# Four weight transfers issued during the attention stage, one ahead of the first gathers, and other places for the last expert's parts

## The chip, the cores and the metric

The kernel runs on one core of a Trainium2 chip. The metric is the device time of one execution, in microseconds (us). The core has five engines that run their own instruction streams: TensorE (PE; its weight loads are shown as PEld), VectorE (DVE), ScalarE (ACT), GpSimd (POOL) and SyncE (SP). Transfers between HBM and SBUF run on 16 DMA engines; here SP issues into the queue that the profile calls q1 and POOL into q0.

## The reference

An attention layer is followed by a mixture of experts with an early exit. What is computed, cut to what matters:

```python
# attention: batch 4, 8 heads, 768 positions, 64 columns a head
scores = scale * np.matmul(q, k.transpose(0, 1, 3, 2))
mask = retrieval heads: causal; the others: causal & (first 4 keys | last 64 keys)
a = softmax(where(mask, scores, -1e9));  attn_out = a @ v
# the rows become x: 3072 tokens x 512
do_compute = (x @ w_skip) > 0            # the other tokens are returned as they are
e_idx = argmax(xc @ w_gate);  gate_w = its softmax probability      # 8 experts
h = np.maximum(xc[mask] @ w1[e], 0.0)    # 512 -> 1024
y[mask] = gate_w[mask, None] * (h @ w2[e])   # 1024 -> 512
out[do_compute] = xc + y
```

## The kernel before

**Attention.** The 32 (batch, head) pairs are taken two heads at a time: 16 pairs, i = 0 to 15. For each, SP loads q and k (384 KB each) into one of four buffers (`load_qk`, line 643); v is loaded for a whole batch (`load_v`, line 653). POOL casts q, k and v to fp16 (lines 689 and 695), PE transposes them, PE forms the scores in blocks, ACT takes the exponential (line 874), PE multiplies with v (line 919) and DVE divides and writes x into SBUF (line 955). A buffer of q or k is loaded again when the cast of the pair four before is done. SP writes x to the output in parts (`x_out`, line 976), the last four of them after the pairs 13, 14 and 15.

**Routing.** The scores of the gates give each chosen token an expert and a slot; each expert has 256 slots, so 16 tiles of 128 slots. The slot table `idx` is ready after a chain of small DVE and PE steps behind the last pair.

**Experts.** For each of the 16 tiles POOL gathers 128 rows of x from the output by an indirect DMA (`gather`, line 1259), DVE casts them, PE transposes them. PE forms the first layer (`first`, line 1315, named F below, with ReLU on ACT) and the second (`second`, line 1337, named Y), DVE adds the result to the rows (line 1343), and POOL scatters them back (line 1272). The gathers wait for all four last writes of x and for `idx`. PE's order is F of an expert, then Y of the one before; at the end Y of expert 5, Y of expert 6, F of expert 7, Y of expert 7.

**Weights.** There are 16 matrices, n = 0 to 15: n = 2e is the first, n = 2e + 1 the second matrix of expert e. Each is 2 MB in fp32. Matrices 0 to 13 are loaded by POOL with a cast to fp16 on the way (`load_weights`, line 478): 0 to 7 in two transfers each, called quarters here (a quarter of an expert's weights, 1 MB read, 512 KB written), and 8 to 13 in one each. They are issued in one fixed order, the list `fill`. Matrices 0 to 8 have places of their own in `wpool`, 9 and 14 in the buffers of v, the others in memory that attention gives back. Matrices 14 and 15 are loaded by SP in fp32, in five parts ((14,0), (14,1), (15,0) and two halves of (15,1)), and cast by ACT and DVE (`load_last`, line 1378, and `cast_last`, line 1385). Each fp32 part needs 8 KB in each partition; it takes the place of a matrix that is used up. `STAGE` says of which: after the whole first layer of that expert for an even number, after both tiles of its second layer for an odd one. SP issues the parts in order, so a part that waits holds those behind it.

**What sets the order.** All work up to the end is entered into a small planner (`Plan`) as operations with an engine, an estimated duration, the names it depends on, and a key. The planner lays them out in time and writes each engine's instructions in that order; on the chip only the data dependencies hold, so the planner's times matter only through the order. Transfers use up time on one engine called Q in the plan: `dma(name, engine, issue, took, ...)` enters an issue on the engine and a transfer of `took` on Q. An issue with `fill` = f may be laid out only when the work planned on Q ends within f us; an issue without `fill` is laid out as soon as its dependencies are met. `quiet` is a list of pairs (a, b): between the start of a and the start of b no issue that has a `fill` is laid out. Before the change there is one pair: from the division of pair 13 (`("Nx", 13)`) to `("r", 1, "glo")`, a step of the routing.

The lines the change touches are those of `dma(("ld", w, i)...)`, `dma(("ldv", b)...)`, the loop over `fill`, the table `STAGE` and the list `pl.quiet`.

Of the kernel before, what the change touches and what calls it, by code (L numbers as in the profile page):

```python
# [15 lines left out]
ACT = mybir.ActivationFunctionType  # L16
# [3 lines left out]
H = 8  # L20
# [32 lines left out]
class Plan:  # L53
# [20 lines left out]
    def dma(self, name, eng, issue, took, fn, deps=(), key=0.0, first=False,  # L74
            lat=1.9, fill=None):
        self.op((name, "go"), eng, issue, fn, deps, key, fill=fill)
        self.op(name, "Q", took, None, [(name, "go")], 0 if first else 1,
                lat=lat)
# [310 lines left out]
def kernel(  # L389
# [64 lines left out]
    NPRE = 9  # L454
# [3 lines left out]
    def wtile(n, pool, **kw):  # L458
        e, half = divmod(n, 2)
        wts[e, half] = pool.tile([P, DS * F], FP16, name=f"w{half + 1}_{e}", **kw)  # L460
# [8 lines left out]
    WHOLE = set(range(8, 15))  # L469

    def load_weights(n, u):
        e, half = divmod(n, 2)
        c = slice(0, DS * F) if n in WHOLE else slice(u * DS * F // 2, (u + 1) * DS * F // 2)

        def go():
            if n in IN_V and u == 0:
                wtile(n, ldv_pool, tag="vf", bufs=2)
            nc.gpsimd.dma_start(out=wts[e, half][:, c],
                                in_=(w1r, w2r)[half][e][:, c])
        return go  # L480

    def slab(shape, dt, name):
        return ldv_pool.tile(shape, dt, tag="vf", bufs=2, name=name)

    with tc.tile_pool(name="sm", bufs=1) as sm_pool, \
# [25 lines left out]
        pl = Plan()  # L511
        op, dma = pl.op, pl.dma
# [125 lines left out]
        def load_qk(i, w, eng):  # L638
            def go():
                b, hs = heads(i)  # L640
                t = ldq_pool.tile([P, 2, NQB, D], FP32, tag=w + "f", bufs=NLD,
                                  name=w + "f")
                eng.dma_start(out=t.rearrange("p h n d -> p h (n d)"),
                              in_=rows6[w][b, :, hs[0]:hs[0] + 2])
                qk32[w, i] = t
            return go

        def load_v(b, h0, h1):
            def go():
                if h0 == 0:  # L650
                    v32[b] = slab([P, H * NQB, D], FP32, "vf")
                c = slice(h0 * NQB, h1 * NQB)
                nc.sync.dma_start(out=v32[b][:, c], in_=rows1["v"][b][:, c])
            return go
# [3 lines left out]
        for i in range(NPR):  # L658
            for w in "qk":
                act = i == 0 and w == "k"  # L660
                dma(("ld", w, i), "ACT" if act else "SP", 0.45, 1.07,
                    load_qk(i, w, nc.scalar if act else nc.sync),
                    [("C" + w, i - NLD)], -95 if act else next(sp))
            if i == 0:
                dma(("ldv", 0), "SP", 0.45, 2.2, load_v(0, 0, 2), (), next(sp))
            elif i == 1:
                dma(("ldv", 0, 1), "SP", 0.45, 4.1, load_v(0, 2, H), (), next(sp))
            elif i % 4 == 3 and i // 4 + 1 < B:
                b = i // 4 + 1
                dma(("ldv", b), "SP", 0.45, 5.3, load_v(b, 0, H),  # L670
                    [("Cv", 4 * b - 5)], next(sp))


# [317 lines left out]
        for i in range(NPR):  # L991
            b = i // 4
# [183 lines left out]
        for ph, c0, n, k0, last in ((0, 0, 18, 140, ("Gs", 2)),  # L1176
# [7 lines left out]
            w = n * 0.008  # L1184
# [162 lines left out]
        for t in range(0, NT, 2):  # L1347
# [3 lines left out]
        fill = [("W", n, u) for n in range(2 * E)  # L1351
                for u in range(1 if n in WHOLE else 2)]
        fill = [f for f in fill if f[1] < 2 * E - 2]
        for x, name in enumerate(fill):
            dma(name, "POOL", 0.58, 5.1 if name[1] in WHOLE else 2.65, load_weights(*name[1:]),
                [("Cv", 1), (fill[x - 1], "go") if x else None,
                 *(place.get(name[1], ["swap"]) if name[1] >= NPRE else [])],
                -60 + x, first=True, fill=1.5 if name[1] < NPRE else 3.0)
        for t in range(NT):
            dma(("G", t), "POOL", 1.25, 0.4, gather(t),  # L1360
                [("z", t // 2 * 2), "idx", *X3],
# [1 line left out]


        CW = DS * F // 4
        STAGE = {(14, 0): 12, (14, 1): 9, (15, 0): 8, (15, 1): 7}

        def load_last(n, u, c0, c1):
            def go():
                at = STAGE[n, u]  # L1370
                if n in IN_V and u == 0:
                    wtile(n, ldv_pool, tag="vf", bufs=2)
                if c0 == 0:
                    kw = dict(tag="vf", bufs=2) if at in IN_V else dict(tag=f"w_{at}")
                    w32[n, u] = (ldv_pool if at in IN_V else wpool if at < NPRE else M.w).tile(
                        [P, 2 * CW], FP32, name=f"w32_{n}_{u}", **kw)
                c = 2 * u * CW
                nc.sync.dma_start(out=w32[n, u][:, c0:c1],
                                  in_=(w1r, w2r)[n % 2][E - 1][:, c + c0:c + c1])
# [12 lines left out]
        for n in (14, 15):  # L1392
            for u in range(2):
                e, half = divmod(STAGE[n, u], 2)
                parts = 2 if (n, u) == (15, 1) else 1
# [89 lines left out]
        for part, (m, after) in enumerate(((3, [("PV", NPR - 1, 1)]),  # L1485
                                           (1, [("r", 0, "slots"), "swap"]),
                                           (6, [("r", 1, "slots"), "swap"]))):
            for n in range(m):
                op(("warm", part, n), "PE", 0.85, warm(part),
                   after + ([("warm", part, n - 1)] if n else []), 0)  # L1490
        pl.quiet = [(("Nx", 13), ("r", 1, "glo"))]
        with tc.manual_schedule():
            pl.write(tps=2)

# [39 lines left out]
```

## Time and profile before

| what | us |
|---|---|
| median of three runs (192.09, 192.97, 202.09) | 192.97 |
| the profiled execution | 191.98 |
| its span, first to last instruction | 190.4 |
| PE busy | 157.8 |
| POOL busy | 125.3 |
| first weight transfer issued by POOL | 62.1 |
| tenth weight transfer issued | 92.3 |
| first gather issued | 107.3 |
| first layer of expert 0 begins | 114.0 |
| last matmul ends | 182.5 |

All times inside an execution are counted from the start of the span. In a timeline a line gives start, duration, engine, line of the kernel, operation, the tiles it writes and reads, and in brackets how long the engine had stood idle and what it had waited for. A table of stretches gives for each stretch the busy time of PE, PEld, DVE, ACT and POOL, then the clock that PE was granted (1.00 is full), then the mean busy share of the 16 DMA engines (it can come out some per cent over 1) and the GB/s moved. In the profile, the bytes of a weight transfer are those written, half of those read.

The ten writes of x, the 22 weight transfers by POOL, the five by SP and the 16 gathers and scatters can each be found by the line that issues them. POOL issues the weight transfers number 11 and 12 (matrix 5) at 102.35 and 104.24 us, ahead of the first gather; number 13, (6,0), follows the second gather.

### The profile page before, as it was taken

To read this page: it belongs to the slowest core of one execution; us is meant where nothing else is said; L and a number is where in the kernel's file an instruction comes from. 1 tells how busy PE (TensorE), PEld (TensorE's weight loads), DVE (VectorE), ACT (ScalarE), POOL (GpSimd) and SP (SyncE) were. 2 spreads that over 40 slices of the span, in tenths; PEclk is the share of its full clock that TensorE was granted. 3 is DMA by queue.
4 is the path that set the end of the run, shared out by engine and by line. 5 is a ranking of instruction groups with operands and counts; after the bars stand their busy time and mean duration, and the time that the engine had idled before them with its cause. 6 is when DMAs were issued, how large, how long until landed. Compare 5 with 4: busy or idle time off the path is not lost.

```text
span 190.4 us, 4704 instructions
## 1 busy us (share of the span) xinstructions
PE 157.8 (83%) x1859; PEld 121.7 (64%) x1874; DVE 115.6 (61%) x249; ACT 103.8 (55%) x136; POOL 125.3 (66%) x211
## 2 busy tenths in 40 slices
PE   0596689998999999999966959699999996995930
PEld 0365678777888888788843428389678673734610
DVE  6738675969797888799988241565673433152320
ACT  2187329986799979989739903136133150423700
POOL 7545997699898999998588488887735234016040
PEclk9999969999999999999999997999999999998795
DMA  5999999988997999999999989999999999899510
GB/s 151 323 312 365 335 362 354 282 288 311 310 356 247 351 284 275 211 216 293 272 237 308 197 159 198 269 258 227 195 236 233 215 261 269 186 406 314 192 65 13
DMA packets 28384, 49.21 MB, mean 258 GB/s; under 512 B 5172, under 2 KB 21428, under 8 KB 27202
## 3 DMA queue, kind: packets, MB, share of 16 engines
q0 software_dynamic: 5728, 19.45, 47.0%
q1 hardware_dynamic: 21296, 28.97, 45.7%
q10 hardware_dynamic: 1330, 0.41, 0.9%
q8 instruction: 16, 0.26, 0.5%
q14 instruction: 14, 0.11, 0.2%
HBM read 56.64 MB, written 10.49 MB: 353 GB/s over the span
## 4 chain that ended last, share of the span: by engine, by line
PE 46%; DMA 18%; issue 13%; DVE 10%; POOL 6%; ACT 4%; POOLq 0%; ACTq 0%; DVEq 0%
PE pst L864 13%; DMA w<-in_moe_w_dram 8%; PE opsa L919 8%; DMA xg<-out_dram,idx 6%; PE pst L852 6%; PE hps L1315 6%; PE yps L1337 5%; PE tps L714 5%; POOL out_dram L1272 3%; DVE k L748 3%; ACT at L874 3%; DMA qf<-in_q_dram 2%; PE tps L725 2%; DMA out_dram<-x 2%; DVE vT L768 1%
## 5 line engine op out<-in xcount | busy, mean ns | idle before, releaser
L874 ACT ACTIVATE at<-pst 128x1024 f16<-128x1024 f32 (+1 forms) x60 | 58.3, 1013 | 14.7 <-PE pst L864 13.8
L1326 ACT ACTIVATE ht<-hps 128x512 f16<-128x512 f32 x32 | 19.1, 597 | 41.4 <-PE hps L1315 30.6
L1272 POOL DMA_INDIRECT out_dram<-xg,idx x16 | 16.6, 1034 | 33.4 <-DVE xg L1343 30.1
L864 PE MATMUL pst<-qT,k 128*128 128x128 f16 (+2 forms) x308 | 36.4, 239 | 2.4 <-ACT qT L740 0.9
L1315 PE MATMUL hps<-xT,w 128*128 128x256 f16 x256 | 33.0, 290 | 4.5 <-ACT w L1385 2.2
L1315 PEld LDWEIGHTS <-w 128*128 128x128 f16 x256 | 29.9, 147 | 7.9 <-ACT w L1385 2.9
L748 DVE COPY k<-tps 64x768 f16<-64x768 f16 x32 | 30.4, 951 | 6.3 <-PE tps L714 5.9
L864 PEld LDWEIGHTS <-k 128*128 128x128 f16 x308 | 24.7, 100 | 11.3 <-issue 2.6
L1337 PE MATMUL yps<-w,ht 128*128 128x512 f16 x128 | 29.1, 379 | 0.0
L1343 DVE SCALAR_TENSOR_TENSOR xg<-yps,gsl,xg 128x512 f32<-128x512 f32 x16 | 11.9, 749 | 16.8 <-PE yps L1337 16.7
L1259 POOL DMA_INDIRECT xg<-out_dram,idx x16 | 17.3, 1078 | 7.1 <-issue 3.7
L919 PE MATMUL opsa<-va,at 128*128 128x74 f16 x392 | 20.2, 199 | 1.5 <-DVE x L955 1.5
L1337 PEld LDWEIGHTS <-ht 128*128 128x128 f16 x128 | 12.2, 98 | 13.0
L919 PEld LDWEIGHTS <-at 128*128 128x128 f16 x472 | 18.6, 99 | 2.0 <-DVE x L955 1.8
L740 ACT COPY qT<-tps 128x768 f16<-128x768 f16 x16 | 12.8, 800 | 7.2 <-PE tps L714 7.2
L852 PE MATMUL pst<-smask,identb 128*128 128x512 bf16 (+3 forms) x49 | 16.2, 344 | 0.3 <-ACT at L874 0.2
L1286 DVE CAST x<-xg 128x512 f16<-128x512 f32 x16 | 10.0, 646 | 10.0 <-issue 5.6
L695 POOL CAST va<-vf 128x768 f16<-128x768 f32 x16 | 13.3, 830 | 2.2 <-PE opsa L919 1.1
L955 DVE TENSOR_TENSOR x<-opsa,recs 128x768 f32<-128x768 f32 x15 | 14.2, 945 | 0.0
L714 PE MATMUL tps<-ident,q 128*128 128x128 f16 x96 | 8.3, 224 | 7.1 <-DVE q L689 6.1
L759 POOL COPY kx<-k 64x256 f16<-64x256 f16 x20 | 8.0, 399 | 8.1 <-DVE k L748 7.4
L1306 DVE COPY xT<-xtp 128x512 f16<-128x512 f16 x16 | 6.3, 421 | 11.5 <-PE xtp L1295 11.2
(139 smaller groups left out, 254.6 us busy)
## 6 DMA issues: line engine op xcount, KB each, us to landing
w<-in_moe_w_dram POOLq DMA_DIRECT2D x16, 512.0 KB, 8.0
qf<-in_q_dram SPq DMA_DIRECT2D x16, 384.0 KB, 6.5
w<-in_moe_w_dram POOLq DMA_DIRECT2D x6, 1024.0 KB, 11.1
kf<-in_k_dram SPq DMA_DIRECT2D x15, 384.0 KB, 6.0
out_dram<-x SPq DMA_DIRECT2D x7, 768.0 KB, 9.4
w<-in_moe_w_dram SPq DMA_DIRECT2D x3, 1024.0 KB, 7.9
w<-in_moe_w_dram SPq DMA_DIRECT2D x2, 512.0 KB, 13.8
kf<-in_k_dram ACTq DMA_DIRECT2D x1, 384.0 KB, 4.8
```

What stands on the lines that cost most here:

```text
L714: nc.tensor.matmul(t[:, n], c16[w, i][:, n].rearrange("p h d -> p (h d)"), C.ident, is_transpose=True, start=(n == 0), stop=(n == NQB - 1))
L748: nc.vector.tensor_copy(to, ti)
L852: nc.tensor.matmul(pst[:, c0 - c * CH:c0 - c * CH + m].rearrange("p (n c) -> p n c", c=P), identb, mv, start=(n == 0), stop=(n == last))
L864: nc.tensor.matmul(pst[:, c0 - c * CH:c0 - c * CH + m * P], lt, qTs[i][:, qb * P:(qb + m) * P], start=(n == 0), stop=(n == last))
L874: nc.scalar.activation(ats[i][:, c * CH:c * CH + cn], psts[i, c][:, :cn], ACT.Exp, scale=SCALE)
L919: nc.tensor.matmul(opss[i][:, hi, qb * VA:(qb + 1) * VA], ats[i][:, b0 + c:b0 + c + P], vb, start=(n == 0), stop=(n == len(todo) - 1))
L955: nc.vector.tensor_mul(xsb[i // 4][:, :, h0 * D:(h0 + 2) * D].rearrange("p n (h d) -> p h n d", h=2), summed(i, GX, 512 - GX, D), recs[:, ...
L1259: h = nc.gpsimd.indirect_dma_start(out=M.xgs[:, t], out_offset=None, in_=out[:, :], in_offset=bass.IndirectOffsetOnAxis(ap=idx[:, t:t + 1] ...
L1272: h = nc.gpsimd.indirect_dma_start(out=out[:, :], out_offset=bass.IndirectOffsetOnAxis(ap=idx[:, t:t + 1], axis=0), in_=M.xgs[:, t], in_of ...
L1315: nc.tensor.matmul(hps[:, fi, :], w1[:, s, 2 * f2 + fi], xTs[e][:, s, :], start=(fi == 0 and s == 0), stop=(fi == 1 and s == DS - 1))
L1326: nc.scalar.activation(hts[e][:, 2 * f2:2 * f2 + 2], hpss[e, f2], ACT.Relu)
L1337: nc.tensor.matmul(ypss[t], hts[e][:, j, s2 * P:(s2 + 1) * P], w2[:, j], start=(j == 0), stop=(j == FS - 1))
```

## The change

- The planner's cost of a load of q or k goes from 1.07 to 0.95, of a batch of v from 5.3 to 4.9.
- The first four quarters, (0,0), (0,1), (1,0) and (1,1), depend on the k casts of the pairs 5, 7, 9 and 11, have no `fill`, and a planned cost of 2.0 in place of 2.65. Their key is below those of POOL's other work, so each follows its cast directly.
- The other quarters of the matrices 2 to 4 get a `fill` of 2.0 in place of 1.5; 5 to 8 keep 1.5, and 9 to 13 keep 3.0.
- A second pair in `quiet`: from the issue of quarter (6,0) to the issue of the second gather nothing with a `fill` is laid out.
- `STAGE`: part (14,0) goes to the place of matrix 10 (free after F of expert 5) instead of 12 (F of expert 6); (15,0) goes to 12 instead of 8 (F of expert 4). (14,1) stays with 9 (Y of expert 4), (15,1) with 7 (Y of expert 3).

```diff
             for w in "qk":
                 act = i == 0 and w == "k"
-                dma(("ld", w, i), "ACT" if act else "SP", 0.45, 1.07,
+                dma(("ld", w, i), "ACT" if act else "SP", 0.45, 0.95,
...
-                dma(("ldv", b), "SP", 0.45, 5.3, load_v(b, 0, H),
+                dma(("ldv", b), "SP", 0.45, 4.9, load_v(b, 0, H),
...
+        EARLY = (5, 7, 9, 11)
         for x, name in enumerate(fill):
-            dma(name, "POOL", 0.58, 5.1 if name[1] in WHOLE else 2.65, load_weights(*name[1:]),
-                [("Cv", 1), (fill[x - 1], "go") if x else None,
+            dma(name, "POOL", 0.58, 5.1 if name[1] in WHOLE else 2.0 if x < len(EARLY) else 2.65, load_weights(*name[1:]),
+                [("Cv", 1), ("Ck", EARLY[x]) if x < len(EARLY) else None, (fill[x - 1], "go") if x else None,
                  *(place.get(name[1], ["swap"]) if name[1] >= NPRE else [])],
-                -60 + x, first=True, fill=1.5 if name[1] < NPRE else 3.0)
+                -60 + x, first=True,
+                fill=(None if x < len(EARLY) else 2.0 if name[1] < 5 else
+                      1.5 if name[1] < NPRE else 3.0))
...
-        STAGE = {(14, 0): 12, (14, 1): 9, (15, 0): 8, (15, 1): 7}
+        STAGE = {(14, 0): 10, (14, 1): 9, (15, 0): 12, (15, 1): 7}
...
-        pl.quiet = [(("Nx", 13), ("r", 1, "glo"))]
+        pl.quiet = [(("Nx", 13), ("r", 1, "glo")),
+                    ((("W", 6, 0), "go"), (("G", 1), "go"))]
```

## The prediction

> **What bounds the kernel now.** I read the page's busy shares and slices first, then a table of short stretches, then PE's instructions in order of time, and last the two DMA queues in half microseconds.
>
> ```profile
> PE 157.8 (83%) x1859; PEld 121.7 (64%) x1874; DVE 115.6 (61%) x249; ACT 103.8 (55%) x136; POOL 125.3 (66%) x211
> DMA  5999999988997999999999989999999999899510
> ```
>
> PE is busy for 83%, but the DMA engines are full in nearly every slice from 5 to 178 us. So moving a transfer gains only if it fills a gap, or if it changes which data lands first. The gaps that could take weights earlier are in the stage that loads q, k and v (columns: PE, PEld, DVE, ACT, POOL busy, clock, DMA share, GB/s):
>
> ```profile
> 40.00:42.00 2.00, 1.87 (x30) 1.29 (x27) 1.97 (x3) 1.08 (x2) 2.00 (x3) 1.00 0.79 261
> ...
> 44.00:46.00 2.00, 1.95 (x50) 1.88 (x49) 1.97 (x4) 1.98 (x3) 1.97 (x4) 1.00 0.63 236
> ...
> 58.00:60.00 2.00, 2.00 (x38) 1.79 (x36) 1.70 (x2) 2.00 (x3) 1.28 (x4) 1.00 0.42 94
> ```
>
> They leave 0.42 + 0.74 + 1.16, some 2.4 us with a little more around 38 us. The other wide gap (0.68 at 34 to 36 us) ends before the first early quarter can be issued. After 62 us no stretch is free: 70 to 80 and 80 to 90 us show shares of 1.07 and 1.05.
>
> The end is set by PE, which waits there for weights:
>
> ```profile
> 155.21 3.62 PE L1337 MATMUL yps<-w,ht 128*128 128x512 f16 x16
> 160.62 3.71 PE L1315 MATMUL hps<-xT,w 128*128 128x256 f16 x32 [1.79 <-DMA w<-in_moe_w_dram]
> 164.16 7.07 PE L1337 MATMUL yps<-w,ht 128*128 128x512 f16 x32
> 171.48 0.44 PE L1315 MATMUL hps<-xT,w 128*128 128x256 f16 x2 [0.25 <-ACT w L1385]
> 173.86 5.16 PE L1315 MATMUL hps<-xT,w 128*128 128x256 f16 x30 [1.94 <-ACT w L1385]
> 178.86 3.62 PE L1337 MATMUL yps<-w,ht 128*128 128x512 f16 x16
> ```
>
> The reader sees expert 6 begin 1.8 us late, and the first layer of expert 7 take from 171.48 to 178.86, that is 7.4 us, where expert 6's took 3.5 (160.62 to 164.16). Of these 3.9 us, 1.94 is waiting for the fp32 parts and their casts, and the rest a granted clock of 0.77 over 171 to 178 us. The fp32 parts are asked for late: SP waits 3.7 us for the end of expert 6's first layer, issues all five from 164.41, and they land from 170.3 to 180.3 us.
>
> **The early quarters.** After the k casts of pairs 5, 7, 9 and 11 on POOL (they end at 37.2, 44.4, 52.0 and 58.2 us) one quarter each is issued. On POOL this is 4 x 0.59 us where it is busy 9.63 of 10 us; casts and copies queue behind it, and through them PE's transposes. Later issues go away, but until the gathers there are 13 quarters instead of 12. Bounds: nothing (in 20 to 62 us PE's waits for POOL come to 0.2 us) to 2.4 us (all four on the path). I take 0.5, near the waits.
>
> On the DMA engines a quarter costs 2.4 us (0.41 to 0.43 MB moved per 2 us between 80 and 86 us, for 0.52 MB). Loads behind it land later by what the gaps don't take. The tightest are the k load of pair 8 (issued 35.2, landed 39.9, cast 45.1) and of pair 11 (45.45, 52.7, 57.4): 5.2 and 4.7 us of cover, against 2.4 and, after two quarters less the gaps at 40 and 44 us, 3.7 us. Later loads have 8 to 12 us. So no cast waits; the cover being gone would cost 2.4 us for each quarter more. The cheaper entries for loads and v are costs of the planner alone: they issue no instruction, only order moves. I take no time from the planner, and count its reordering within the 0.5.
>
> **The gathers.** POOL's order there is now:
>
> ```profile
> 102.35 0.59 POOL L478 DMA_DIRECT2D w<-in_moe_w_dram  x1
> ...
> 104.24 0.59 POOL L478 DMA_DIRECT2D w<-in_moe_w_dram  x1
> 107.31 1.09 POOL L1259 DMA_INDIRECT xg<-out_dram,idx  x1 [2.49 <-PE hps L1480]
> 108.70 1.03 POOL L1259 DMA_INDIRECT xg<-out_dram,idx  x1 [0.30 <-issue]
> ```
>
> The second silence takes one of the two quarters away. That frees little: POOL is waiting anyway until the slot numbers are ready at 106.2 us, and the second gather lands 3.2 us after its issue, the shortest of all gathers. Expert 0 needs both, so the gain at its start is under 0.3 us. But the gathers also wait for the last writes of x. The last is issued at 101.81 and lands 4.3 us later, at 106.1, level with the slot numbers. By the time the first silence begins, ten quarters have been issued now and twelve afterwards (thirteen, if (6,0) still slips in). Two more are 4.8 us of DMA work, and the gaps took 2.4. The rest stands before the last writes. How the two queues share shows in 87.0 to 87.5 us, where both have work:
>
> ```profile
> q0 software_dynamic: 20, 0.08, 80.8%
> q1 hardware_dynamic: 15, 0.03, 18.0%
> ```
>
> POOL's weights (q0) take four fifths and SP's writes (q1) one fifth. So the last writes, and the gathers, come 2.4 us later; bounds -0.3 (all hidden, one quarter less ahead) and +4.8 (thirteen). I take 2.4. With the 0.5, expert 0 starts 2.9 us late. PE's wait of 1.61 us for the fifth gather, at 122.73, is then covered: the DMA work ahead of that gather is a quarter further on, so it lands no later than now (121.95), while PE comes later. Expert 1's first layer starts at 124.69 + 2.9 - 1.6 = 126.0.
>
> From there PE runs without a break to where expert 6 is ready: 158.83 + 1.3 = 160.1 us. The DMA order after the gathers is the old one, a quarter ahead, so matrix 12 lands 2.4 us before its 160.62 when alone. The 1.8 us wait goes, and what is late next is PE itself: gain 0.5.
>
> **The last expert's parts.** No instruction is added; four places change, so waits on SP do. Part (14,0) takes the place of expert 5's first matrix, free at 154.8 instead of 164.1 us; (14,1) follows at 158.8 (its place is as before, but it no longer queues behind a wait for expert 6); (15,0) takes expert 6's place at its end, and (15,1), behind it, a place long free. So two parts, 2.5 us of DMA each (0.84 MB in 2 us at 168 to 172), run beside matrices 12 and 13 on POOL's queue, both needed sooner. A packet of a part takes 275 ns (120 packets in 168 to 170 us at 103% of 16 engines), one of a whole matrix about 500 (66 in 156 to 158 us at 104.7%). The share of 80.8% above fits turns of one packet each (291 ns a packet of a quarter, 79 ns one of the writes), so the matrices keep 500/775, about 65%. The trace doesn't show parts and matrices together with both full; bounds 25% and 100%, I take 65%. Matrix 12 then lands at 160 at most. Matrix 13, 164.2 us alone (166.6 less 2.4), lands at about 167.5.
>
> The Trainium skill ("DMA: Bandwidth & Descriptors", Queues, rings and completion order) says each DMA engine goes round its queues packet by packet, a packet holding some 9 to 17 descriptors. "Trainium Kernel Development and Optimization", Key Constraints, adds that a second issuing engine saves only issue time, which speaks against this edit: the parts bring no bandwidth of their own. By these rules with equal bytes in a packet the share would be a half and matrix 13 some 2 us later; the trace's 80.8% against 18.0% goes against equal turns by bytes.
>
> **The sum.** Expert 6's first layer 160.1 to 163.6, expert 5's second to 167.2, expert 6's second from 167.5 to 171.1, expert 7's first with (14,*) cast by then 3.5 us to 174.6, its second 3.6 to 178.2. The parts of matrix 15 land by 180.3 - 2.4 - 1.0 (the engines stand 39% idle in 164 to 166 us, and more around it) = 176.9, cast by 177.5, in time for the last quarter. I add 1.2 us for a clock that still dips after a short wait (expert 7 paid 1.7 now). PE ends at 179.4 instead of 182.48: 3.1 us less. The scatters behind it stay. The profiled execution took 191.98 us (span 190.4, 1.6 around it), so 188.9; the median of the three runs shown lies 1.0 above that execution and the lowest at 192.09, so I set half a microsecond on it: **189.4 us**.
>
> **Rivals.** *All hidden* (chance 0.15): the last writes aren't delayed and matrices keep their queue; -2.4 at the start, and PE is limited by its own work: about 186.7. For it: the loads' cover. Against it: full shares after 62 us. *The wait only moves* (0.20): expert 7 no longer waits, but expert 6's second layer waits for matrix 13 as long, with the clock dip; 190.5 to 194, centre 192. For it: the DMA engines are full at both ends. *The parts starve the matrices* (0.20): at a share of 25%, matrix 12 lands at 163 and 13 at 174; then second layer to 177.6, expert 7 to 184.6, 1.7 for the clock and 0.5 for POOL: 186.8, or +4.3, 196.8 us on the median's scale, 196 to 199. It decides from a share below one half. For it: 1.7 us of full SP queue at 70 to 72 us with POOL's nearly still; against it: the 80.8%. That the first silence lets thirteen quarters pass, so that the second does nothing new, moves 2.4 us at the gathers, and the tail takes most of it back; it is within the forecast.
>
> **Numbers.** The forecast has 0.45, with its own range 187.4 to 191.4. More than 2% faster (about what a measurement of this kernel can tell from no change) is under 189.1: a bit over half of the forecast and all of *all hidden*, 0.40. Slower by over 2%: most of *starve*, 0.15. The rest is 0.45. The range leaves out half of *all hidden* and half of *starve*: 186.6 to 197.0.
>
> **What would show it.** Right: four weight issues between 37 and 59 us; casts of k not waiting for loads; first gather at 109 to 110; SP's first part issued near 156; no wait over 1 us before expert 7. Wrong: a first gather at 107 (no backlog), matrix 13 landing after 171 with PE waiting before expert 6's second layer, attention ending over 2 us later, or DMA gaps that stay open at 40 to 60 us.

## The result

The changed kernel takes 198.47 us (median of 22 executions, 194.76 to 201.29) against 195.68 us for the kernel before, measured beside it (22 executions, 189.22 to 202.09). Some executions of both were disturbed; over the others the ratio is 1.028, with a 95% interval of 1.022 to 1.034. The change makes the kernel slower, where 189.4 us was predicted.

The profiled execution took 195.07 us (span 193.6), 3.1 us more than the one before. The ratio stands for some 5 us, so these two executions lie closer together than the kernels do; the table accounts for the 3.1. Where these came in, by points of the two profiles:

| point | before, us | after, us | later by |
|---|---|---|---|
| last product with v begins its last matmul | 98.00 | 105.00 | 7.0 |
| first layer of expert 0 begins | 113.96 | 122.92 | 9.0 |
| first layer of expert 6 begins | 160.62 | 166.55 | 5.9 |
| last matmul ends | 182.48 | 185.44 | 3.0 |

So attention loses 7.0 us, the routing 2.0, and the experts give 6.0 back. The busy line and the DMA slices of the changed kernel's page:

```profile
PE 157.5 (81%) x1859; PEld 122.0 (63%) x1874; DVE 118.4 (61%) x249; ACT 103.6 (54%) x136; POOL 124.2 (64%) x211
...
DMA  5999999899999999999999683999999999999420
```

PE does the same work and stands still for longer. The DMA engines are full for the first 106 us, and then a hole has come (6, 8 and 3, at 106 to 121 us). The stretches of the load stage show what the quarters did (columns as in the table of stretches before):

```profile
40.00:42.00 2.00, 1.75 (x26) 1.17 (x23) 1.94 (x4) 1.08 (x2) 2.00 (x4) 1.00 0.96 227
44.00:46.00 2.00, 1.95 (x48) 1.88 (x48) 1.97 (x4) 1.86 (x3) 2.00 (x4) 1.00 1.01 345
...
58.00:60.00 2.00, 2.00 (x41) 1.76 (x40) 1.99 (x4) 1.57 (x2) 1.96 (x4) 1.00 1.01 223
...
68.00:70.00 2.00, 0.63 (x9) 0.33 (x6) 1.90 (x5) 0.00 (x0) 0.18 (x1) 1.00 1.04 330
70.00:72.00 2.00, 0.00 (x0) 0.00 (x0) 1.12 (x2) 0.00 (x0) 1.88 (x4) 1.00 1.05 350
```

The gaps are filled: 0.79, 0.63 and 0.42 have become 0.96, 1.01 and 1.01. But at 68 to 72 us PE and ACT stand still with the DMA engines full. The timeline of POOL says for whom:

```profile
59.09 0.53 POOL L478 DMA_DIRECT2D w<-in_moe_w_dram  x1
...
62.22 0.83 POOL L695 CAST va<-vf 128x768 f16<-128x768 f32 x1
69.81 0.83 POOL L689 CAST k<-kf 128x768 f16<-128x768 f32 x1 [6.77 <-DMA kf<-in_k_dram]
```

POOL waits 6.77 us for the k load of pair 12. In the kernel before that cast began at 62.82 us with no wait:

```profile
62.82 0.85 POOL L689 CAST k<-kf 128x768 f16<-128x768 f32 x1
```

SP's timeline, first of the kernel before and then of the changed one, shows the load itself:

```profile
48.55 1.34 SPq L643 DMA_DIRECT2D kf<-in_k_dram  x1
50.11 0.71 SPq L653 DMA_DIRECT2D vf<-in_v_dram  x1
```

```profile
48.57 1.93 SPq L653 DMA_DIRECT2D vf<-in_v_dram  x1
50.74 13.56 SPq L643 DMA_DIRECT2D kf<-in_k_dram  x1
```

Two things have changed. The planner put v of batch 3 ahead of k of pair 12 (the cheaper costs alone make it do so, and so do the four quarters with the old costs, as two of the runs below show). And the issue of k holds SP for 13.56 us. The load landed 6.2 us after its issue before, and lands 18.9 us after it now (at 69.7 instead of 54.8 us).

### The profile page after: what moved, and what is told of

Read it like the earlier page. It is cut to its first block, busy times and chain, and to the rows that moved or that the text cites. A ratio compares the mean times of both kernels' runs of the same rounds, so it can differ in the third digit from the quotient of the medians.

```text
span 193.6 us, 4701 instructions
## 1 busy us (share of the span) xinstructions
PE 157.5 (81%) x1859; PEld 122.0 (63%) x1874; DVE 118.4 (61%) x249; ACT 103.6 (54%) x136; POOL 124.2 (64%) x211
## 5 line engine op out<-in xcount | busy, mean ns | idle before, releaser
L864 PEld LDWEIGHTS <-k 128*128 128x128 f16 x308 | 25.0, 101 | 12.4 <-issue 3.6
L1315 PE MATMUL hps<-xT,w 128*128 128x256 f16 x256 | 31.5, 282 | 1.3 <-ACT w L1389 0.8
L1315 PEld LDWEIGHTS <-w 128*128 128x128 f16 x256 | 29.4, 145 | 3.7 <-ACT w L1389 1.0
L1337 PE MATMUL yps<-w,ht 128*128 128x512 f16 x128 | 29.7, 379 | 0.1
L1259 POOL DMA_INDIRECT xg<-out_dram,idx x16 | 16.5, 1031 | 7.4 <-issue 4.0
L1343 DVE SCALAR_TENSOR_TENSOR xg<-yps,gsl,xg 128x512 f32<-128x512 f32 x16 | 11.9, 750 | 12.9 <-PE yps L1337 12.4
L689 POOL CAST k<-kf 128x768 f16<-128x768 f32 x15 | 12.4, 828 | 6.9 <-DMA kf<-in_k_dram 6.8
L740 ACT COPY qT<-tps 128x768 f16<-128x768 f16 x16 | 12.8, 798 | 7.1 <-PE tps L714 7.1
L768 DVE COPY vT<-tps 128x768 f16<-128x768 f16 x16 | 8.8, 549 | 9.6 <-PE tps L725 9.6
```

Of the source, the lines that this page charges most:

```text
L864: nc.tensor.matmul(pst[:, c0 - c * CH:c0 - c * CH + m * P], lt, qTs[i][:, qb * P:(qb + m) * P], start=(n == 0), stop=(n == last))
L1259: h = nc.gpsimd.indirect_dma_start(out=M.xgs[:, t], out_offset=None, in_=out[:, :], in_offset=bass.IndirectOffsetOnAxis(ap=idx[:, t:t + 1] ...
L1315: nc.tensor.matmul(hps[:, fi, :], w1[:, s, 2 * f2 + fi], xTs[e][:, s, :], start=(fi == 0 and s == 0), stop=(fi == 1 and s == DS - 1))
L1337: nc.tensor.matmul(ypss[t], hts[e][:, j, s2 * P:(s2 + 1) * P], w2[:, j], start=(j == 0), stop=(j == FS - 1))
```

## The experiments

### One load put back in its order

My first theory was the order: v, with its many packets, had come ahead of k of pair 12.

```diff
-                    [("Cv", 4 * b - 5)], next(sp))
+                    [("Cv", 4 * b - 5), (("ld", "k", 12), "go") if b == 3 else None], next(sp))
```

> The changed kernel with one dependency more: SP issues v of batch 3 after k of pair 12, as in the kernel before; the four early quarters, the second silence and the new places stay. Theory (k of pair 12 is late because it stands behind v of batch 3 on SP, and v is slow because quarters run beside it): POOL's wait of 6.8 us for k disappears, the first layer of expert 0 begins near 116 instead of 122.9 us, and the kernel is 3 to 5 us faster than before, since the tail's gain of 5.8 us stays. Rival (the early quarters take DMA time that the loads need, whatever the order): POOL waits about as long for another load, v of batch 3 or q of pair 13, and the kernel stays 2 to 5 us slower than before.

The wait for k of pair 12 went, and others came. The two fastest of four executions took 195.04 and 196.89 us, no less than the changed kernel's lowest (194.76). In the profiled one (196.89) the last product with v began its last matmul at 108.40 us, 3.4 later than in the changed kernel, and expert 0 started at 123.97. POOL's timeline:

```profile
71.93 0.82 POOL L689 CAST q<-qf 128x768 f16<-128x768 f32 x1 [1.13 <-DMA qf<-in_q_dram]
...
89.51 0.82 POOL L689 CAST q<-qf 128x768 f16<-128x768 f32 x1 [7.53 <-DMA qf<-in_q_dram]
```

Now q of pair 13 and q of pair 15 are late. The second was issued at 70.78 us and landed 18.6 us later, while POOL issued five quarters between 69.45 and 80.01. So the order alone doesn't explain the loss. The opposite edit, on the kernel before, agrees:

```diff
-                    [("C" + w, i - NLD)], -95 if act else next(sp))
+                    [("C" + w, i - NLD), (("ldv", 3), "go") if (w, i) == ("k", 12) else None],
+                    -95 if act else next(sp))
```

> The kernel before with one dependency more: SP issues k of pair 12 after v of batch 3. No early quarters. Theory (order and quarters together make the wait): v issues and moves in its old 10 us, k of pair 12 lands some 10 to 13 us after its issue near 49, at 60 to 62, and is cast at 62.8, so POOL waits under 1.5 us and the time is within 1% of before. Rival (the order alone does it): POOL waits 5 us or more and the kernel is 2.5% slower.

With v ahead of k and no early quarter, the ratio to the kernel before is 1.005 (0.996 to 1.013). No cast waits. But the order isn't free: k of pair 12 landed at 60.4 us, 5.6 later than before, and was cast at 61.94. It had 8.1 us of cover and has 1.6 left.

### Two early quarters in place of four

```diff
-        EARLY = (5, 7, 9, 11)
+        EARLY = (5, 7)
```

> The changed kernel with two early quarters instead of four (after the k casts of pairs 5 and 7); the others go by the planner's fill, the third behind v of batch 3. SP's order stays that of the change, with v of batch 3 ahead of k of pair 12. Theory (v is slow because quarters take DMA turns from its small packets): v lands some 10 to 13 us after its issue instead of 20, POOL's wait for k falls from 6.8 to under 2 us, and the kernel is 1 to 4 us faster than before. Rival (the order alone does it): the wait stays at 5 us or more.

The ratio is 1.014 (1.003 to 1.025), between none and four. POOL waits 4.76 us for k of pair 12, which was issued at 50.65 us and landed 17.0 later, at 67.7. Three quarters were issued before that (36.60, 44.45 and, by the planner's own rule, 61.04). Beside the run without early quarters, with the same order of loads, these are prices: three quarters delayed this load from 60.4 to 67.7, by 7.3 us, and the four of the changed kernel to 69.7, by 9.3 us. Two quarters ahead of it, in the run with the costs alone further down, delayed it to 64.6, by 4.2. Each figure is from one profiled execution; with four quarters there are six in all, and the load landed at 68.6 to 69.8 us. **So each quarter delays it by some 2.1 to 2.4 us, nearly all of the 2.4 us that a quarter takes on the DMA engines.** How that comes about is seen in the two queues of the changed kernel, at 58 to 60 us (packets, MB, share of 16 engines):

```profile
q0 software_dynamic: 84, 0.33, 80.8%
q1 hardware_dynamic: 110, 0.12, 20.3%
```

SP's loads get more packets through than POOL's quarters, and a fifth of the time, since one of their packets takes 59 ns (20.3% of 32 us over 110) and one of a quarter 308 ns. At 50 to 52 us it is 85 packets with 83.6% against 84 with 23.6%. The Trainium skill ("DMA: Bandwidth & Descriptors", Queues, rings and completion order) has the engines go round their queues packet by packet, and the packet counts agree with it, those at 50 to 52 us closely, those at 58 to 60 us roughly.

### One early quarter

One quarter, after the k cast of pair 9, on the kernel before, with the planner's cost of a quarter as it was:

```diff
+            EARLY = (9,)
...
+                [("Cv", 1), ("Ck", EARLY[x]) if x < len(EARLY) else None, (fill[x - 1], "go") if x else None,
...
+                fill=None if x < len(EARLY) else 1.5 if name[1] < NPRE else 3.0)
```

> The kernel before with a single early quarter, after the k cast of pair 9 (near 52 us), at the old costs; the planner leaves SP's order, and nearly all of PE's and POOL's, as before. Theory (about 1 quarter fits the gaps of 2.4 us and the cover of the loads): no POOL wait for a load over 1 us, the gap at 58 to 60 us is filled, and the time is within 1% of before, up to 1.5 us faster. Rival (a quarter beside v holds the loads however few there are): POOL waits 2 us or more for k of pair 12 or q of pair 13, and the time is 1% or more above before.

The fastest of its four executions took 190.74 us (the fastest of the kernel before: 190.59 to 192.4); there is no ratio. The same kernel once more:

> The kernel before with one early quarter after the k cast of pair 9 (the same kernel as the run with one quarter, which had too few undisturbed executions to say). Theory: the gaps of the load stage come to 2.4 us, one quarter fits into them, no cast waits for a load, and the tail has one quarter less to wait for; but 11 instead of 10 quarters stand ahead of the last writes of x, which land some 2 us later. So the two cancel: 190 to 193, a ratio of 0.99 to 1.005. Rival (each early quarter costs its whole 2.4 us): 194 to 195, a ratio of 1.01 to 1.015. Third: the gain at the end stays, 188 to 190, a ratio under 0.99, and one quarter would beat both kernels.

The ratio is 0.999 (0.988 to 1.010). The expected backlog before the gathers didn't come either: the second quarter is issued at 67.85 us, where the kernel before issued it at 69.29, and the tenth at 92.34 (92.29 before). The rule `fill` took back what the early quarter brought. The first gather is at 107.21 (107.31 before). One quarter costs the loads nothing that shows (no cast waits for one), and what it gains or loses is within some 1%.

### The planner's costs

The costs alone, on the kernel before:

```diff
-                dma(("ld", w, i), "ACT" if act else "SP", 0.45, 1.07,
+                dma(("ld", w, i), "ACT" if act else "SP", 0.45, 0.95,
...
-                dma(("ldv", b), "SP", 0.45, 5.3, load_v(b, 0, H),
+                dma(("ldv", b), "SP", 0.45, 4.9, load_v(b, 0, H),
```

> The kernel before with only the planner's cheaper loads (0.95 and 4.9 instead of 1.07 and 5.3). No instruction changes, but the order does: the planner, which now sees room, issues two quarters during the loads, after the casts of pair 5 and 6, and v of batch 3 ahead of k of pair 12. Theory (each quarter beside the loads costs them some 2.4 us, and the planner's belief in cheaper loads is part of the harm): POOL waits 2 to 5 us for a load, expert 0 begins 2 to 5 us later than before, and the time is 1 to 2.5% above before. Rival (only the four quarters entered by hand harm): no wait over 1 us, time within 1% of before.

The ratio is 1.041 (1.024 to 1.058), 198.48 us by the median of four. With loads that look cheaper the planner lays two quarters at 38.82 and 44.09 us by itself, and twelve instead of ten before the first silence. POOL waits only 1.2 us for loads. But the last two of the twelve are issued at 92.97 and 95.29, right ahead of the last writes of x, and these land 11.0 to 12.4 us after their issue (the last one 4.3 us before). POOL's timeline:

```profile
107.08 0.58 POOL L478 DMA_DIRECT2D w<-in_moe_w_dram  x1
116.84 1.08 POOL L1259 DMA_INDIRECT xg<-out_dram,idx  x1 [9.19 <-issue]
```

The slot numbers are ready at 109.0 us, and the first gather still comes at 116.84. The page gives this wait to "issue"; among those who waited for the writes of x, the trace names POOL's gather with 9.2 us. That the two quarters more are what delays the writes is argued and not shown. With ten quarters ahead of them, as before, the last write also landed 9.0 us after its issue in the profiled execution with v ahead of k (196.25 us), and 7.9 in that of the first run with one quarter (199.34 us); the gathers came 5.9 and 4.8 us after the slot numbers there.

Then the costs taken out of the changed kernel:

```diff
-                dma(("ld", w, i), "ACT" if act else "SP", 0.45, 0.95,
+                dma(("ld", w, i), "ACT" if act else "SP", 0.45, 1.07,
...
-                dma(("ldv", b), "SP", 0.45, 4.9, load_v(b, 0, H),
+                dma(("ldv", b), "SP", 0.45, 5.3, load_v(b, 0, H),
```

> The changed kernel with the planner's old costs for loads (1.07 and 5.3). SP's order is that of the changed kernel, v of batch 3 ahead of k of pair 12; on POOL the fifth and the seventh quarter change places with casts and copies beside them. Theory (quarters beside loads, whatever the costs): the four early quarters are issued as in the changed kernel, POOL waits 5 to 8 us for k of pair 12 or for a load behind it, and the time is that of the changed kernel within 1.5 us: 197 to 200 by the median, a ratio of 1.02 to 1.035. Rival (the cheaper costs, which alone made the kernel before 4% slower, are what makes the changed kernel slow): 192 to 195, a ratio under 1.015.

The ratio is 1.044 (1.036 to 1.052), above that of the changed kernel. SP's order is the same: the four quarters alone put v ahead of k. POOL waits 6.04 us for k of pair 12 and 0.74 for pair 11, and expert 0 starts at 125.28. So the costs are not what makes the changed kernel slow; with four forced quarters they help, if anything. No run has the four quarters and nothing else of the change; this is the nearest.

### The tail

The new places of the parts alone, on the kernel before:

```diff
-        STAGE = {(14, 0): 12, (14, 1): 9, (15, 0): 8, (15, 1): 7}
+        STAGE = {(14, 0): 10, (14, 1): 9, (15, 0): 12, (15, 1): 7}
```

> The kernel before with only the new places of the last expert's parts. Theory (the tail's gain in the changed kernel comes from these places): PE's wait inside the first layer of expert 7 falls from 1.9 us to under 1, matrix 12 is no earlier, and the time falls by 1 to 3 us. Rival (the tail gained only because the weights had 7 us more time while attention was late): PE waits as before, or for matrix 12 or 13 instead, and the time is within 1 us of before. Rival of the prediction (the parts starve the matrices): PE waits 3 us or more ahead of expert 6's second layer and the time rises by 2 us or more.

The profiled execution took 194.29 us, another one 194.97, against 189.5 to 191.8 of the fastest of the kernel before beside it; there is no ratio. SP issues the first part at 153.77 us instead of 164.41, and matrix 12 lands 18.9 us after its issue, at 163.5 instead of 160.6. PE, and the two queues at 160 to 162 us:

```profile
163.50 6.23 PE L1315 MATMUL hps<-xT,w 128*128 128x256 f16 x32 [5.92 <-DMA w<-in_moe_w_dram]
```

```profile
q1 hardware_dynamic: 67, 0.51, 60.9%
q0 software_dynamic: 57, 0.25, 44.5%
```

Expert 6 waits 5.9 us instead of 1.8. SP's parts take 61% of the time and POOL's queue 44%, for 67 packets against 57: again nearly equal turns. But POOL's queue carries more than matrices. Of its 57 packets 15 are of 8 KB, a matrix's, at 624 ns each, and 30 of 4 KB at 159 ns, the scatters' (12 hold 4 bytes). So the matrices got 29% of the time (38% from 157.0 to 163.5 us), where the prediction had 65%, and the scatters 15%. Then the old places in the changed kernel:

```diff
-        STAGE = {(14, 0): 10, (14, 1): 9, (15, 0): 12, (15, 1): 7}
+        STAGE = {(14, 0): 12, (14, 1): 9, (15, 0): 8, (15, 1): 7}
```

> The changed kernel with the old places of the last expert's parts. Theory (the parts' earlier issue takes DMA time from the matrices; the tail is short in the changed kernel only because the weights had the 7 us more by which attention is late): expert 6 doesn't wait, the parts are issued after expert 6's first layer, PE waits 1 to 4 us for them ahead of expert 7, and the time is 0 to 3 us above the changed kernel. Rival (the new places harm here too): the time is 1 us or more below the changed kernel.

The ratio is 1.026 (0.996 to 1.057): too wide to tell it from the changed kernel. Its two fastest executions took 194.65 and 197.29 us, those of the changed kernel 194.76 to 197.14. What `STAGE` is worth there stays open.

### The second silence

```diff
-        pl.quiet = [(("Nx", 13), ("r", 1, "glo")),
-                    ((("W", 6, 0), "go"), (("G", 1), "go"))]
+        pl.quiet = [(("Nx", 13), ("r", 1, "glo"))]
```

> The changed kernel without the second silence: two quarters ahead of the first gather again. Theory (the silence changes little at the gathers, and the DMA engines' idle time of some 6 us between 108 and 120 us is a consequence of the late attention): expert 0's first layer begins within 0.7 us after the first gather lands as in the changed kernel, and the time is within 1% of the changed kernel. Rival (the idle DMA time is what the changed kernel pays): 2 us or more faster than the changed kernel.

The ratio rises to 1.048 (1.039 to 1.056), all four executions above 198.9 us. I had expected next to nothing. The gathers of expert 0 land 3.6 to 4.8 us after their issue, behind two quarters, and 2.2 to 3.3 us behind one, and DVE, whose order has the third gather's cast ahead of the second one's last copy, waits 1.94 us for that as well; expert 0 starts 21.4 us after the last product with v instead of 17.9. PE's line:

```profile
127.01 3.36 PE L1315 MATMUL hps<-xT,w 128*128 128x256 f16 x15 [2.48 <-DVE xT L1306]
```

So this part of the change helps, by 3.5 us at this point: 1.4 because the second gather lands later, and 2.0 by DVE's order behind it. In all it is worth 1 to 2% (1.048 beside 1.028, and beside 1.035 when the changed kernel's order was measured once more, below).

### The two microseconds in the routing

Between the last product with v and expert 0 the changed kernel needs 17.9 us, the kernel before 16.0. DVE's timeline, and POOL's, of the changed kernel:

```profile
104.59 1.98 DVE L1146 TENSOR_TENSOR r_a<-r_r,r_b 128x18 f16<-128x18 int32 x1
...
107.54 0.35 DVE L945 TENSOR_TENSOR lgh<-opsa,recs 128x108 f32<-128x108 f32 x1
```

```profile
104.40 2.13 POOL L1117 TENSOR_TENSOR tables<-r_oht,val 128x1152 f16<-128x1152 f16 x1 [3.40 <-DVE r_r L1113]
```

A subtraction of 18 numbers in each partition takes 1.98 us, where it took 0.37 before:

```profile
96.81 0.37 DVE L1146 TENSOR_TENSOR r_a<-r_r,r_b 128x18 f16<-128x18 int32 x1
```

In the changed kernel it ends at 106.57, and the POOL step that runs beside it at 106.54. The last pair's `lgh`, on which the routing hangs, stands behind it on DVE: it follows the last product by 2.5 us, before by 0.5. Other runs agree. Where `r_a` takes 1.98 us and one quarter stands ahead of the gathers (this kernel, the old costs, the old places and the next run) expert 0 starts 17.9 to 18.0 us after the last product; with k of pair 12 put first `r_a` takes 0.37 us and it is 15.6, with two early quarters 0.18 us and 16.0. The first attempt to part the two named a wait in the planner:

```diff
-                   f[nm], [("r", ph, "glo"), ("r", ph, "oht")] if r_ else prev,
+                   f[nm], [("r", ph, "glo"), ("r", ph, "oht" if ph else "oa")] if r_ else prev,
...
```

> The changed kernel with one wait more and every engine's order as it was: POOL's long table step (line 1117, 2.13 us) waits for DVE's r_oa instead of r_oht, so that it no longer runs beside DVE's r_a. Of the 9.0 us by which expert 0 starts later than before, the k wait explains 7.0 (end of the last product with v). Theory: the other 2 us are r_a, which takes 1.98 us in the changed kernel instead of 0.37 because POOL's step started 0.19 us ahead of it and it ends 0.04 us after POOL's; DVE's lgh of the last pair stands behind it. Then r_a takes 0.2 us here, lgh follows the last product by 0.7 instead of 2.5 us, and the first gather is issued 1.0 to 1.8 us earlier than at 116.49 (POOL's three steps of line 1127 now follow its table step directly and end some 0.3 us later, which takes part of the gain). Expert 0 starts at 121.1 to 122.0 instead of 122.92, and the time falls by 1 to 1.5 us against the changed kernel: 196.5 to 197.5 by the median, a ratio of 1.02 to the kernel before. Rival: r_a is long for another reason (its data, the x step before it), it still takes 1.98 us, and nothing moves.

The planner's order stayed as it was, and since its names make no waits on the chip, this was the changed kernel once more: `r_a` 1.98 us, 197.62 us by the median, a ratio of 1.035 (1.026 to 1.043). It says how far two runs of one order differ: here pair 11's k waits too (3.25 us, then 4.52 for pair 12), expert 0 starts at 123.52, and PE waits 2.46 us for matrix 13. Ratios within 1% of each other are thus not told apart here. The next one changed POOL's order:

```diff
-                   f[nm], [("r", ph, "glo"), ("r", ph, "oht")] if r_ else prev,
+                   f[nm], [("r", ph, "glo"), ("r", ph, "oht") if ph else ("r", 0, "L", 0)] if r_ else prev,
...
-                   [("r", ph, "r16" if ph else "oa")], k0 + 0.3)
+                   [("r", ph, "r16" if ph else "R" if m else "oa")], k0 + 0.3)
...
```

> The run before this one named a wait only to the planner, whose order stayed the same; so on the chip nothing waited, and it was the changed kernel over again. Here POOL's order itself is changed, and nothing else: its first table step of line 1127, which reads DVE's r_oa and r_ob, stands ahead of the 2.13 us table step of line 1117, so no POOL step can run beside r_a. Theory (DVE's r_a, 1.98 us instead of 0.37, is held by the POOL step beside it): r_a takes 0.2 us, lgh of the last pair follows the last product with v by 0.7 to 0.9 instead of 2.5 us, and the first layer of expert 0 starts 17.0 to 17.6 us after the last product instead of 17.9 (the POOL steps, moved back by nothing, end as late as before and take part of the gain); by the median 196.5 to 198, 0 to 1.5 us under the changed kernel. Rival: r_a still takes 1.98 us, and the interval from the last product to expert 0 stays 17.9.

DVE's timeline:

```profile
105.78 0.18 DVE L1146 TENSOR_TENSOR r_a<-r_r,r_b 128x18 f16<-128x18 int32 x1
...
110.53 1.33 DVE L1101 TENSOR_TENSOR val<-r_gate,val 128x6 f16<-128x6 f32 x1
```

`r_a` takes 0.18 us and `lgh` follows the last product by 0.7 us, as expected. But now `val` (1.33 us) and `r_h` (1.05) run beside POOL's other table steps, PE waits 1.28 us for the last of them, and the slot numbers are ready 11.0 us after the last product instead of 10.5. Expert 0 starts 19.0 us after it, where 17.0 to 17.6 was expected. Nothing is won: the lowest of four executions took 196.75 us, and there is no ratio. The cause of the long step is shown, a better order was not found.

## Why the prediction was wrong

From the start of expert 0 to PE's last matmul I had 116.9 to 179.4, 62.5 us; the profile has 122.92 to 185.44, 62.5 us. All of the 6.2 us between 188.9 and 195.07 stands ahead of expert 0 but for 0.2.

- **"So no cast waits" was the step that failed**, and with it the 0.5 us for the stage: 7.0. I set the cover of each load against one or two quarters and stopped at "Later loads have 8 to 12 us". The tightest of these is k of pair 12, with 8.1 us, and all four quarters stand ahead of it. In the runs the order of v and k took 5.6 us of that cover and the four quarters 9.3: 14.9 us, of which 8.1 were covered and 6.8 were POOL's wait. The gaps of 2.4 us, which I took off, saved this load next to nothing. My own numbers, 9.6 less 2.4, come to 7.2, close to the 7.0 lost, but that is chance: against 8.1 us of cover 7.2 would not have been late. I brought forward the sum of the delays to the last writes of x, and not to the loads ahead of them.
- **"Count its reordering within the 0.5"** failed too. The order of v and k used up 5.6 of those 8.1 us; alone it costs nothing measurable (1.005), under the quarters it decides which load is late first. It comes with the cheaper costs and with the four quarters alike. And the costs alone, taken by me for a matter of order only, make the kernel before some 4% slower in the four executions measured; in the profiled one the gathers wait for the last writes, with two more quarters ahead of these.
- **The gathers "2.4 us later" by the last writes**: gathers do wait for these writes, 9.2 us in the run with the costs alone, but not in the changed kernel. There the last write is issued at 110.8 us and lands 3.3 later, at 114.2, ahead of the slot numbers (115.5): attention came so late that the DMA engines had run out of work (the 6 and the 8 in their slices). First gather: 116.49 instead of 109 to 110.
- **The routing** was not a step of mine at all; it costs 2.0 us. DVE's `r_a` beside POOL's table step makes the slot numbers 2.4 us later, counted from the last product. The second gather lands 1.3 us sooner after them, and 0.9 goes to DVE, which now does the whole of the first tile ahead of the second one's cast. So the error is 6.5 (casts) + 2.0 (routing) - 2.4 (last writes) = 6.1 us.
- **"The gain at its start is under 0.3 us"** for the second silence was too little: without it expert 0 is 3.5 us later after the last product, 1.4 of it by the gathers. I had read it from a kernel in which the gathers landed 3.2 to 4.5 us after their issue with two quarters ahead, and took that for the floor; with one quarter it is 2.2 to 3.3.
- **The tail** came out at 62.5 us, but not by my working. PE in the changed kernel:

```profile
166.55 3.66 PE L1315 MATMUL hps<-xT,w 128*128 128x256 f16 x32
170.04 7.45 PE L1337 MATMUL yps<-w,ht 128*128 128x512 f16 x32
177.33 0.38 PE L1315 MATMUL hps<-xT,w 128*128 128x256 f16 x2
178.48 3.50 PE L1315 MATMUL hps<-xT,w 128*128 128x256 f16 x30 [0.77 <-ACT w L1389]
181.82 3.62 PE L1337 MATMUL yps<-w,ht 128*128 128x512 f16 x16
```

No wait for matrix 12 or 13 and 0.77 us for the parts, as predicted. But I let the matrices keep 65% beside the parts, by turns of one packet each and a mean packet of POOL's queue, and forgot that the scatters take some of that queue's turns. In the run with the new places alone the matrices got 29 to 38%, and expert 6 waited 5.9 us: the rival *The parts starve the matrices*, with matrix 12 at 163.5 us where it gave 163. In the changed kernel this doesn't show. There PE is ready for expert 6 at 166.55 us instead of 158.83 and matrix 12 is issued as much later (153.75 instead of 145.91), but it lands in under 12.8 us instead of 14.7, before SP's parts (from 162.90) can slow it by much; matrix 13 lands at 173.7, just when it is needed. The same order once more took 64.3 us here, with 2.46 for matrix 13, and two early quarters took 66.4, so part of the agreement is luck. How the 6.0 us divide between the quarters brought forward and the new places stays open, since the run with the old places was too uncertain.

Two slips of mine change nothing in the sum. `STAGE` changes two places, not four. And by the lines shown for 87.0 to 87.5 us a packet takes 323 and 96 ns (80.8% and 18.0% of 8 us, over 20 and 15), not 291 and 79; the shares come out alike.

The rival that ended on the slow side put the loss in the tail. It was in the loads.

## What to carry to other kernels

When transfers are brought forward into a stage, add up all that stand ahead of a load, with what a changed order costs it, and set the sum against its cover, not each one against the load beside it. Don't count on the gaps: here they saved the tightest load next to nothing. Where two queues are busy, ask which kinds of packet each holds and how long each kind takes before guessing shares: the queue with the long packets takes the time. And a change of a planner's costs is a change of the order on every engine; compare the orders instruction by instruction before pricing it at nothing.

## What was not expected of the hardware

- A small DVE step can last as long as the POOL step beside it. `r_a` ended 0.03 us after POOL's table step in the changed kernel (106.57 and 106.54) and in the kernel before (97.17 and 97.14), and took 0.18 us with no POOL step beside it. DVE's conversion of `val` (6 numbers in a partition) took 0.91 us in the changed kernel and ended at 111.82, POOL's step at 111.79; in the kernel before it took 0.56. Of 0.94 us of DVE work from PSUM (`x`, line 955) beside the same POOL step nothing was lost. The Trainium skill ("SBUF — State Buffer", Who interferes with whom) says that a DVE instruction with two inputs in SBUF, or one in a mode with two ports, excludes a GpSimd instruction that reads SBUF, and that the later of the two waits for the end of the other; the runs agree for `r_a`, which has two. Which mode `val`'s conversion runs in, no run here shows.
- An issue on SP can hold SP for long. The load issued right behind v of batch 3 held it for 7.45 us in the kernel before (q of pair 13), 8.73 with k of pair 12 there, and 13.56 with the four quarters besides; k of pair 12 ahead of v took 1.34.
- The mean time of a packet says little when a queue holds several kinds. A matrix's packet of 8 KB took 625 ns without SP's parts (the kernel before, 156 to 158 us) and 624 ns beside them (the run with the new places alone, 160 to 162 us). The mean over POOL's queue fell from 508 to 250 ns, since more packets of the scatters (4 KB, some 160 ns) stood between.
